# Second copy buffer in the gradient stage, four kernel-gradient rows, other places of loads, stores and jobs in a fused H3 and SiLU training step

## The chip, the cores and the metric

The kernel runs on one core of a Trainium2 chip. A core has a matrix engine (TensorE, in the profile PE, its weight loads PEld), a vector engine (VectorE, DVE), a scalar engine (ScalarE, ACT), GpSimd (POOL) and SyncE (SP), which here only issues DMAs. Each engine works through its own instructions in order; semaphores tie the engines together. DMAs are issued from the queues of SP, ACT and POOL and share 16 DMA engines. The metric is the device time of one execution in microseconds; lower is better.

## The reference

It is a forward pass of two layers and its vector-Jacobian product, with S = 2048 rows, D = 448 channels and F = 1792 hidden channels, in bfloat16:

```python
def _A_ref(q, k, v, shift_k, ssm_k, ssm_D):        # sequence mixing
    k_shift = sum(k_pad[:, t:t+S] * shift_k[:, ks-1-t] for t in range(4))
    kv = k_shift * v
    y = irfft(rfft(pad(kv)) * rfft(pad(ssm_k)))[:S] + kv * ssm_D
    return q * y
def _B_ref(x, w1, w2):                             # dense layer
    return silu(x @ w1) @ w2
x = A_q
for layer in range(2):
    x = x + _A_ref(_layernorm(x), A_k, A_v, A_shift_k, A_ssm_k, A_ssm_D)
    x = x + _B_ref(_layernorm(x), B_w1, B_w2)
```

This is shortened; the layer norm has no weights. The outputs are `x` and the gradients, for a given `grad_out`, of `q`, `k`, `v`, `shift_k`, `ssm_k`, `ssm_D`, `w1` and `w2`. The convolution's result `y` is the same in both layers, since `k`, `v` and the kernels are.

## The kernel before, in words

The work has three parts.

The prefix, `_ssm_prefix` (about the first 100 us), computes `y`: a Fourier transform of length 4096 as two stages of matmuls with constant matrices (`M1s`, `Gsb`, `Minvs`). It leaves the spectra in HBM (`spec_K`, `spec_KV`) and `y` in SBUF. `Gsb` is loaded once, into a pool that lives as long as the kernel.

The middle, `Main.run`, works in chunks `c` of 512 rows, four in each layer. Forward layer 0 comes first, then a loop over layer 1's chunks that does the second half of `h` (the product with `w1`, L518 through `contract`), `out` (the product with `w2`, L600), and then already the backward part of the same chunk. Then comes a loop over layer 0's chunks with the backward part only. The backward part of a chunk has two functions:

- `ga` (L618) makes the gradient that goes through `w2`. In seven pairs of F tiles `fp`, TensorE runs 8 matmuls of 512 columns into the tile `ps_g`, ACT copies it to SBUF as `ghp` (L626), and DVE multiplies `ghp` by the slope of SiLU, `dT`, into `ghT` (L634). `ps_g` has two buffers, `ghp` one. `mid` and `slope` put further ACT or DVE work between the pairs.
- `gn` (L662) runs 56 matmuls `ps_n` with `w1T` (L672), which ACT moves out as `lb_u` (L674), and then the backward pass of two layer norms (`ln_bwd`, lines 640 to 660), almost all of it on DVE (`lb_junk`, `lb_cc`, `lb_u`, `G`, `gy`), with `lb_v` on ACT (L652).

At the head of a chunk stands `g_pre`. It loads the output gradient `gb` (in layer 1, from SP's queue) and transposes it on TensorE into `gT`. In `contract` the argument `at` decides whether the half-height blocks of a product stand first or last: it is compared with 0 only.

The suffix, `_ssm_suffix`, does two things at once. It runs the sequence mixing backwards: stage 1 of the transform (`_fft_stage1`, 16 columns `n2`, moved out as `A1g`, the first twelve on ACT), transposes, spectra (`spectrum`, `inverse`), the gradient of `ssm_k` (L969 to L993: four rows `gK` of 112 channels, each made by two groups of 16 matmuls, copied by ACT or DVE, then stored), that of `k` and `v` (L998 on), and the sums for `gk` on DVE. Between these, it weaves the *jobs*, the weight gradients: 56 jobs of 16 matmuls `ps_d` (L808), each of which loads a tile `dstat` of 512 KB on SP's queue. `weave(n)` puts `n` job matmuls between two steps of the transform, and `_in_turn` keeps TensorE's order as written. A pair of jobs makes one tile of 128 rows: `_gw2` for `w2` (moved out as `dout`, stored from POOL's queue, L823), `_gw1` for `w1` (also transposed, `do`, L835 to L838). Where the weaving is over, the rest of the jobs follow one another to the end.

The order inside each engine's queue is decided by a scheduler when the program is built: it may draw an instruction ahead of others when its data and buffers allow, unless the code pins it (`issue_after`, `_in_turn`, `high_priority`). A pool's tile with a `tag` and `bufs=n` takes turns among `n` places; a new tile waits until the last reader of the old one in its place is done. `k.bal` keeps a running estimate of the loads of ACT and DVE and gives a copy to the one with less.

Of the kernel before, what the change touches and what calls it, by code (L numbers as in the profile page):

```python
# [10 lines left out]
FP32 = mybir.dt.float32  # L11
# [108 lines left out]
@with_exitstack  # L120
def kernel(
    ctx: ExitStack,
    tc: tile.TileContext,
    A_q: bass.AP,
    A_k: bass.AP,
    A_v: bass.AP,
    A_shift_k: bass.AP,
    A_ssm_k: bass.AP,
    A_ssm_D: bass.AP,
    B_x: bass.AP,  # L130
    B_w1: bass.AP,
    B_w2: bass.AP,
    grad_out: bass.AP,
    out_0: bass.AP,
    out_1: bass.AP,
    out_2: bass.AP,
    out_3: bass.AP,
    out_4: bass.AP,
    out_5: bass.AP,
    out_6: bass.AP,  # L140
    out_7: bass.AP,
    out_8: bass.AP,
):
    nc = tc.nc
    k = K()
    k.tc, k.nc = tc, nc
    k.bal = _Bal(nc)
    for nm, v in (("A_q", A_q), ("A_k", A_k), ("A_v", A_v), ("A_shift_k", A_shift_k), ("A_ssm_k", A_ssm_k),
                  ("A_ssm_D", A_ssm_D), ("B_w1", B_w1), ("B_w2", B_w2), ("grad_out", grad_out)):
        setattr(k, nm, v)  # L150
    k.outs = [out_0, out_1, out_2, out_3, out_4, out_5, out_6, out_7, out_8]
    C = make_fft_consts()

    dram = ctx.enter_context(tc.tile_pool(name="dram", bufs=1, space=DRAM))
    k.KS_d = dram.tile([S, D], BF16, name="KS_d")
    k.SPEC_d = {nm: dram.tile([128, SPEC], BF16, name=f"spec_{nm}") for nm in ("K", "KV")}
    k.N_d = [dram.tile([S, D], BF16, name=f"N_d{i}") for i in range(4)]
    k.DT_d = dram.tile([4, 2, P, NF // 2, 512], BF16, name="DT_d")
    k.A_d = [dram.tile([P, NF, NT, P], BF16, name=f"A_d{i}") for i in range(2)]
    k.AP_d = dram.tile([4, P, S], BF16, name="AP_d")  # L160
    k.GH_d = [dram.tile([P, NF, NT, P], BF16, name=f"GH_d{i}") for i in range(2)]

    bf = mybir.dt.np(BF16)
    m1b = np.ascontiguousarray(C["M1"], dtype=np.float32).astype(bf)
    minv = (np.transpose(m1b.astype(np.float32), (3, 1, 2, 0)) * np.float32(C["inv_scale"])).astype(bf)
    k.m1_h = nc.inline_tensor(np.ascontiguousarray(m1b.reshape(P, -1)), name="c_m1")
    gs_h = nc.inline_tensor(np.ascontiguousarray(C["Gs"].reshape(P, -1)).astype(np.float32).astype(bf), name="c_gs")
    k.minv_h = nc.inline_tensor(np.ascontiguousarray(minv.reshape(P, -1)), name="c_minv")

    keep = ctx.enter_context(tc.tile_pool(name="keep", bufs=1))  # L170
    k.ident = keep.tile([P, P], BF16, name="ident")
    make_identity(nc, k.ident[:])
    k.Gsb = keep.tile([P, 5, P], BF16, name="Gsb")
    nc.gpsimd.dma_start(out=k.Gsb[:].rearrange("p a k -> p (a k)"), in_=gs_h.ap())
    k.rstd = [keep.tile([P, J], FP32, name=f"rstd{i}") for i in range(4)]
    k.warm = keep.tile([P, 4], FP32, name="warm")
    k.mhalf = keep.tile([P, 4], FP32, name="mhalf")
    nc.gpsimd.memset(k.mhalf[:], -0.5)
    nc.scalar.activation(k.warm[:], k.mhalf[:], ACT.Silu)
    k.wk = ctx.enter_context(tc.tile_pool(name="wk", bufs=1))  # L180
    k.dp = ctx.enter_context(tc.tile_pool(name="dp", bufs=1))
    k.yk = ctx.enter_context(tc.tile_pool(name="yk", bufs=1, side="right", reuse_waits="tile"))
    k.Ysb = k.yk.tile([P, J, D], BF16, name="Ysb", tag="Y")
    _ssm_prefix(k)
    k.w1sb = k.wk.tile([P, ND, F], BF16, name="w1sb", tag="WA")
    nc.sync.dma_start(out=k.w1sb[:, 0:3, :], in_=k.B_w1[0:384].rearrange("(c p) f -> p c f", p=P))
    nc.sync.dma_start(out=k.w1sb[:, 3, :], in_=k.B_w1[320:448])
    k.w2sb = k.wk.tile([P, NF, D], BF16, name="w2sb", tag="WB")
    nc.sync.dma_start(out=k.w2sb[:], in_=k.B_w2.rearrange("(c p) d -> p c d", p=P))
    k.psum = ctx.enter_context(tc.tile_pool(name="psum", bufs=1, space=PSUM, reuse_waits="tile"))  # L190
    k.xg = ctx.enter_context(tc.tile_pool(name="xg", bufs=1, side="right", reuse_waits="tile"))
    k.X = k.xg.tile([P, NT, D], BF16, name="X", tag="X")
    k.gYb = k.xg.tile([P, NT, D], BF16, name="gYb", tag="GY")
    k.bal.reset()
    with ExitStack() as es:
        m = Main(k, es)
        m.run()
    _ssm_suffix(k)


# [80 lines left out]
def _ssm_prefix(k):  # L281
# [4 lines left out]
    with ExitStack() as es:  # L286
# [22 lines left out]
        skc = spec.tile([DC, ND, 4], FP32, name="skc")  # L309
        skb = spec.tile([DC, ND, 4], BF16, name="skb")  # L310
        Drow = spec.tile([1, D], BF16, name="Drow")

        nc.gpsimd.dma_start(out=Drow[:], in_=k.A_ssm_D.rearrange("(o d) -> o d", o=1))
        nc.scalar.dma_start(out=skb[:], in_=k.A_shift_k.rearrange("(c p) j -> p c j", p=DC))
# [149 lines left out]
class Main:  # L464
# [98 lines left out]
    def h(self, c, L, nT, half, hold, pre=None):  # L563
# [2 lines left out]
        dT = self.td.tile([P, NF // 2, 512], BF16, name="dT", tag="D", bufs=3)  # L566
        hold.append((aT, dT))
        d0 = pre() if pre else None
        for ft0, n, at in ((0, 2, 1), (2, 2, 0), (4, 2, None), (6, 1, None)) if half == 0 else ((7, 1, None), (8, 2, 1), (10, 2, 0), (12, 2, None)):
            ps = k.psum.tile([P, 2, 512], FP32, name="ps_h", tag="mm", bufs=2)  # L570
            self.contract(ps, self.w1sb, nT, ft0, n, at)
            o = ft0 - 7 * half
# [30 lines left out]
        if last:  # L603
            nc.gpsimd.dma_start(out=_pm(k.outs[0][0])[:, 4 * c:4 * c + 4, :], in_=X[:, 4 * c:4 * c + 4, :])

    def g_pre(self, c, L):
        nc, k = self.nc, self.k
        sl = slice(4 * c, 4 * c + 4)
        if L == 1:
            gb = self.ch.tile([P, 4, D], BF16, name="gb", tag="gb", bufs=2)  # L610
            nc.sync.dma_start(out=gb[:], in_=_pm(k.grad_out[0])[:, sl, :])
        else:
            gb = k.X[:, sl, :]
        gT = self.ch.tile([P, ND, 512], BF16, name="gT", tag="nT", bufs=2)
        self.transp(gb, gT)
        return gb, gT

    def ga(self, c, L, gT, dT, mid=None, loads=(None, None)):  # L618
# [3 lines left out]
        for fp in range(NF // 2):  # L622
            ps = k.psum.tile([P, 2, 512], FP32, name="ps_g", tag="mm", bufs=2)
            self.contract(ps, self.w2T, gT, 2 * fp, 2, None if fp == 6 else (fp + 1) % 2)
            gh = self.ch.tile([P, 2, 512], BF16, name="ghp", tag="ghp", bufs=1)
            k.last_gh = nc.scalar.copy(gh[:], ps[:])  # L626
            k.bal.add("act", 0.95)
            k.bal.add("dve", -0.5)
# [84 lines left out]
    def run(self):  # L713
# [19 lines left out]
            self.out(c, cur, False)  # L733
            cur = fol
        for c in range(4):
            gb, gT = self.g_pre(c, 1)
            d0 = self.h(c, 1, nT, 1, cur, (lambda: self.load_d(0, 0)) if c == 3 else None)
            if c < 3:
                na1 = self.a_fwd(c + 1, 2, None)
# [1 line left out]
            if c < 2:  # L741
                self.turn_plain(2 * c)
                self.turn_plain(2 * c + 1)
            if c == 3:
                self.slope(d0)
            box = []
# [79 lines left out]
def _gw1(k, pool, slots):  # L826
# [5 lines left out]
    def turn(ft, o):  # L832
        pt = psum.tile([DC, ND, P], BF16, name="ps_dt", tag="po", bufs=2)
        for dc in range(ND):
            nc.tensor.transpose(pt[:, dc, :], o[:, dc * DC:(dc + 1) * DC], k.ident[:])  # L835
        o7 = pool.tile([DC, ND, P], BF16, name="do7", tag="do7", bufs=2)
        nc.scalar.copy(o7[:], pt[:])
        nc.gpsimd.dma_start(out=out7v[:, :, ft * P:(ft + 1) * P], in_=o7[:])  # L838

    hold = None  # L840
    for ft in range(NF):
# [15 lines left out]
def _ssm_suffix(k):  # L857
# [6 lines left out]
    k.pt = dict(s1=mm, s2=mm, v=mm)  # L864
    with ExitStack() as es:
        pool = lambda name: es.enter_context(tc.tile_pool(name=name, bufs=1, reuse_waits="tile"))
        sp = pool("sspec")
        k.Minvsb = sp.tile([P, 16, 2, P], BF16, name="Minvs")
        dp2 = pool("dp2")
        k.tail = None  # L870
        both = [(k.dp, "dstat", 3), (k.dp, "dstat", 3), (dp2, "dstat", 2), (k.dp, "dstat", 3), (dp2, "dstat", 2)]
        for _ in _gw2(k, k.dp, range(1), [(k.dp, "dstat", 3)], first=k.go_jobs.ins):
            pass

        def jobs():
            yield from _gw2(k, k.dp, range(1, 4), [(k.dp, "dstat", 3)])
            yield from _gw2(k, k.dp, range(4, NF), both)
            yield from _gw1(k, dp2, both)

        jobs = jobs()  # L880
# [1 line left out]
        def weave(n):  # L882
            with _in_turn(k):
                for _ in zip(range(n), jobs):
                    pass
        A1 = sp.tile([P, NDH, 2, 16, 4], BF16, name="A1g")
        Z = sp.tile([P, NDH, P], BF16, name="Zg")
        ksf = k.yk.tile([P, J, D], BF16, name="ksf", tag="Y")
        B1k = A1[:].rearrange("p a c n s -> p (a c n s)").rearrange("p (q d) -> p q d", d=D)
        for n2 in range(16):  # L890
            with _in_turn(k):
                _fft_stage1(k, n2, k.gYb[:, n2, :], A1, psum, nc.scalar if n2 < 12 else None)
            weave(4 if n2 < 8 else 8 if n2 < 11 else 10)
        with tc.tile_pool(name="sspec2", bufs=1, reuse_waits="tile") as p1:
            Zf = Z[:].rearrange("p a b -> p (a b)")
            A1f = A1[:].rearrange("p a c n s -> p a (c n s)")
# [64 lines left out]
        for lo, hi in ((1, 113), (113, 128)):  # L961
            nc.scalar.dma_start(out=kx[lo:hi, 0:3, :], in_=k_pm[lo - 1:hi - 1, 13:16, :])
        nc.gpsimd.memset(gkh[:], 0.0)
        sk_all = p2.tile([P, D * 4], BF16, name="sk_all2", tag="gK", bufs=2)
        nc.sync.dma_start(out=sk_all[:], in_=k.A_shift_k.rearrange("d j -> (d j)").partition_broadcast(P))
        skb = p2.tile([P, 4, D], BF16, name="skb2")
        nc.vector.tensor_copy(skb[:], sk_all[:].rearrange("p (d j) -> p j d", j=4))
# [2 lines left out]
        pr = psum.tile([1, ND, DC], FP32, name="ps_r", tag="po", bufs=2)  # L970
        gKs = []
        for dc in range(ND):
            gK = p2.tile([DC, S], BF16, name="gK", tag="gK", bufs=2)
            gKv = gK[:].rearrange("p (n1 n2) -> p n1 n2", n2=16)
            for g in range(2):
                py = psum.tile([P, 8, P], FP32, name="ps_gK", **mm)
# [69 lines left out]
            nc.gpsimd.dma_start(out=o4[1536:1792].rearrange("(b n) -> b n", b=2), in_=gsk[0:2, 3, :])  # L1046
        weave(2 * NF * 2 * NT)
        for g in range(8):
            acc = p2.tile([P, 2, D], FP32, name="gk_acc", tag="gK", bufs=2)
            gk = p2.tile([P, 2, D], BF16, name="gk", tag="gk", bufs=2)  # L1050
            last = None
            for j in range(4):
# [41 lines left out]
```

## Time and profile before

| | us |
|---|---|
| median of 8 runs (lowest to highest) | 770.17 (769.1 to 773.7) |
| the profiled execution | 773.7 |
| its span, first to last instruction | 771.9 |
| TensorE busy | 715.3 (93%) |
| VectorE busy | 509.7 (66%) |
| ScalarE busy | 457.0 (59%) |
| GpSimd busy | 102.5 (13%) |
| chain that ended last | TensorE 36%, VectorE 27%, issue 15%, ScalarE 11%, DMA 6% |
| output gradient `gb`, issue to landing | 4.7 (4 loads of 448 KB, SP) |
| store of a `gK` row, issue to landing | 6.1 (4 stores, POOL) |

In a row of a timeline the first number is the start in the span, the second the duration of the group of instructions, then come the engine, the line, the operation, the result and the operands with their shapes, and the count. In brackets stands how long the engine had been idle just before and what ended that. In a row of the waits stand the engine, tile and line that waited, the one it waited for, the sum in us, how many times, and the longest. TensorE's matmuls are pipelined, so the duration of a group is a little longer than its distance from the next.

### The profile page before, as it was taken

How to read it: one execution, taken by the hardware profiler on the slowest of the kernel's cores; microseconds unless marked ns; L12 is line 12 of the kernel's file. 1: busy time of each engine (PE TensorE's matmuls, PEld its weight loads, DVE VectorE, ACT ScalarE, POOL GpSimd, SP SyncE). 2: the span in 40 equal slices, each digit the busy share in tenths (PEclk: the TensorE clock that was granted, in tenths of full speed). 3: DMA queues.
4: the chain of work that ended last, by engine and by line, in shares of the span. 5: the costliest groups of instructions: out<-in, count | busy, mean ns of one | idle time of the engine just before them, and what ended most of it. 6: DMA issues, size and time to landing. Idle time of an engine off the chain costs nothing.

```text
span 771.9 us, 12680 instructions
## 1 busy us (share of the span) xinstructions
PE 715.3 (93%) x4981; PEld 382.1 (50%) x5025; DVE 509.7 (66%) x1061; ACT 457.0 (59%) x574; POOL 102.5 (13%) x169
## 2 busy tenths in 40 slices
PE   5998779999999999999999999999999989799995
PEld 4876534444444443434444344344666765455553
DVE  3789758788733796966949778886487715169600
ACT  3878867666557587578857678647467645011111
POOL 1134312222100001000000000002011123021111
PEclk9999979999999999999999999999999999899998
DMA  9449989999979998859889999998669786487760
GB/s 291 162 142 275 362 247 307 263 295 266 214 164 236 216 234 206 178 146 250 193 177 274 285 233 274 283 240 296 246 222 354 259 285 205 125 275 230 220 180 18
DMA packets 187623, 180.01 MB, mean 233 GB/s; under 512 B 135242, under 2 KB 163790, under 8 KB 186412
## 3 DMA queue, kind: packets, MB, share of 16 engines
q1 hardware_dynamic: 173808, 121.98, 61.1%
q0 software_dynamic: 12832, 54.70, 20.6%
q10 hardware_dynamic: 924, 2.52, 1.0%
q8 instruction: 39, 0.64, 0.3%
q14 instruction: 20, 0.16, 0.1%
HBM read 76.50 MB, written 65.87 MB: 184 GB/s over the span
## 4 chain that ended last, share of the span: by engine, by line
PE 36%; DVE 27%; issue 15%; ACT 11%; DMA 6%; POOL 3%; SPq 0%; ACTq 0%; POOLq 0%; DVEq 0%
PE ps_d L808 9%; PE ps_o L600 7%; PE ps_h L518 6%; DVE lb_junk L647 4%; DVE dT L113 3%; DVE ghT L634 3%; DVE lb_u L658 3%; ACT ghp L626 3%; PE ps_v L233 2%; DVE lb_u L687 2%; PE ps_n L672 2%; PE ps_v L232 2%; ACT na L274 2%; DVE ln_st L260 2%; DMA KB<-Z 1%
## 5 line engine op out<-in xcount | busy, mean ns | idle before, releaser
L808 PEld LDWEIGHTS <-dstat 128*128 128x128 bf16 x896 | 85.6, 98 | 74.0 <-issue 3.1
L518 PE MATMUL ps_h<-nT,w1sb 128*128 128x512 bf16 (+1 forms) x434 | 102.9, 386 | 5.9 <-DVE dT L113 3.1
L518 PE MATMUL ps_g<-gT,w2T 128*128 128x512 bf16 (+1 forms) x431 | 97.4, 380 | 9.1 <-ACT ghp L626 7.1
L672 PE MATMUL ps_n<-w1T,ghT 128*128 128x448 bf16 x448 | 92.6, 353 | 1.0 <-DVE ghT L634 0.4
L600 PE MATMUL ps_o<-w2sb,aT 128*128 128x448 bf16 x448 | 90.8, 353 | 0.2 <-ACT aT L575 0.2
L808 PE MATMUL ps_d<-mov,dstat 128*128 128x448 bf16 x448 | 87.4, 353 | 0.2 <-DMA mov<-N_d 0.2
L575 ACT ACTIVATE aT<-ps_h 128x1024 bf16<-128x1024 f32 (+1 forms) x64 | 58.2, 917 | 41.3 <-PE ps_h L518 32.6
L626 ACT CAST ghp<-ps_g 128x1024 bf16<-128x1024 f32 x56 | 56.5, 1008 | 37.0 <-DVE ghT L634 22.9
L113 DVE CAST dT<-ps_h 128x1024 bf16<-128x1024 f32 (+1 forms) x56 | 59.2, 1064 | 26.5 <-ACT aT L575 26.5
L518 PEld LDWEIGHTS <-w2T 128*128 128x128 bf16 (+1 forms) x448 | 36.4, 96 | 68.1 <-issue 37.5
L518 PEld LDWEIGHTS <-w1sb 128*128 128x128 bf16 (+1 forms) x448 | 36.5, 97 | 67.8 <-issue 40.0
L672 PEld LDWEIGHTS <-ghT 128*128 128x128 bf16 x448 | 41.5, 98 | 45.4 <-DVE ghT L634 5.7
L600 PEld LDWEIGHTS <-aT 128*128 128x128 bf16 x448 | 42.1, 98 | 42.6 <-issue 4.5
L808 PE MATMUL ps_d<-X,dstat 128*128 128x448 bf16 x224 | 53.5, 364 | 0.1
L808 PE MATMUL ps_d<-GO,dstat 128*128 128x448 bf16 x224 | 51.2, 352 | 0.2
L232 PE MATMUL ps_v<-Gsb,pa 128*128 128x128 bf16 x336 | 43.8, 221 | 5.4 <-DVE pa L442 4.7
L233 PE MATMUL ps_v<-Gsb,pb 128*128 128x128 bf16 x336 | 42.9, 222 | 2.3 <-DVE pb L942 1.1
L852 ACT CAST dout<-ps_d 128x448 bf16<-128x448 f32 x14 | 7.4, 532 | 58.7 <-PE ps_d L808 58.7
L232 PEld LDWEIGHTS <-pa 128*128 128x128 bf16 x336 | 33.2, 99 | 10.5 <-DVE pa L442 6.8
L674 ACT ACTIVATE lb_u<-ps_n,rstd 128x448 f32<-128x448 f32 x32 | 20.3, 634 | 29.6 <-DVE X L659 13.5
L233 PEld LDWEIGHTS <-pb 128*128 128x128 bf16 x336 | 32.9, 99 | 9.3 <-DVE pb L443 4.6
L634 DVE TENSOR_TENSOR ghT<-dT,ghp 128x1024 bf16<-128x1024 bf16 (+1 forms) x32 | 19.5, 620 | 26.9 <-ACT ghp L626 26.9
(189 smaller groups left out, 1172.6 us busy)
## 6 DMA issues: line engine op xcount, KB each, us to landing
GH_d<-turned SPq DMA_DIRECT2D x16, 896.0 KB, 5.4
dstat<-A_d SPq DMA_DIRECT2D x28, 512.0 KB, 5.2
dstat<-GH_d SPq DMA_DIRECT2D x28, 512.0 KB, 3.8
A_d<-turned SPq DMA_DIRECT2D x12, 896.0 KB, 4.6
DT_d<-dT POOLq DMA_DIRECT2D x8, 896.0 KB, 6.0
dTl<-DT_d SPq DMA_DIRECT2D x8, 896.0 KB, 6.3
spec_K<-Z POOLq DMA_DIRECT2D x7, 512.0 KB, 7.6
KB<-Z POOLq DMA_DIRECT2D x14, 256.0 KB, 12.2
```

The source lines that it names most:

```text
L113: eng.tensor_copy(out, in_)
L232: nc.tensor.matmul(pv[:, i, :], lhsT=pa[:, i * P:(i + 1) * P], rhs=k.Gsb[:, ga, :], start=True, stop=False)
L233: nc.tensor.matmul(pv[:, i, :], lhsT=pb[:, i * P:(i + 1) * P], rhs=k.Gsb[:, gb, :], start=False, stop=True)
L518: self.nc.tensor.matmul(ps[:, u, :], lhsT=w[lo:hi, b, f:f + P], rhs=x[lo:hi, b, :], start=(seen[u] == 1), stop=(seen[u] == ND))
L575: last = nc.scalar.activation(a, ps[:, 0:n, :], ACT.Silu)
L600: nc.tensor.matmul(po[:, :D], lhsT=aT[ft // 7][0][:, ft % 7, tl * P:(tl + 1) * P], rhs=self.w2sb[:, ft, :], start=(ft == 0), stop=(ft == N ...
L626: k.last_gh = nc.scalar.copy(gh[:], ps[:])
L634: nc.vector.tensor_tensor(out=ghT[hh][:, o:o + len(u), :], in0=dT[hh][1][:, o:o + len(u), :], in1=gh[:, u[0]:u[0] + len(u), :], op=ALU.mult)
L647: nc.vector.scalar_tensor_tensor(out=junk[:], in0=u0, scalar=1.0, in1=n_t, op0=ALU.mult, op1=ALU.mult, accum_out=cp[:, 1:2])
L658: nc.vector.scalar_tensor_tensor(out=u0, in0=n_t, scalar=cc[:, 1:2], in1=u0, op0=ALU.mult, op1=ALU.add)
L672: nc.tensor.matmul(pn[:, :D], lhsT=ghT[ft // 7][:, ft % 7, tl * P:(tl + 1) * P], rhs=self.w1T[:, ft, :], start=(ft == 0), stop=(ft == NF - 1))
L808: i = k.nc.tensor.matmul(ps[:, :D], lhsT=st[:, t, :], rhs=mov[:, t, :], start=start and t == 0, stop=stop and t == NT - 1)
```

## The change

1. `Gsb` no longer lives as long as the kernel: the prefix loads it into its own pool, and the suffix loads it again (`Gs`), in both cases from POOL's queue.
2. `h` passes `at` as 1 where it passed None.
3. The load of the output gradient becomes a function, `g_load`; layer 1's loop calls it for the next chunk ahead of `ga`, and for the first ahead of the loop's work.
4. `ghp` has two buffers.
5. The last two stores of `w1`'s gradient are issued on SP's queue.
6. In the suffix the pool `dp2` is laid out first, `Minvs` and `Gs` after `A1g`; the jobs rotate over five `dstat` tiles (three in `k.dp`, two in `dp2`) from the second pair on, where that began with the fifth pair.
7. Stage 1 weaves 2 job matmuls after each of columns 0 to 7, 8 after 8 to 11, and 12 after 12 to 15, in all 96, where it had 4, 8 (up to column 10) and 10, in all 106.
8. The tag `gK` (the rows `gK`, before them `sk_all`, after them `gk_acc`) has four places.

```diff
-    k.Gsb = keep.tile([P, 5, P], BF16, name="Gsb")
-    nc.gpsimd.dma_start(out=k.Gsb[:].rearrange("p a k -> p (a k)"), in_=gs_h.ap())
+    k.gs_h = gs_h
...
+        k.Gsb = spec.tile([P, 5, P], BF16, name="Gsb")
+        nc.gpsimd.dma_start(out=k.Gsb[:].rearrange("p a k -> p (a k)"), in_=k.gs_h.ap())
...
-        for ft0, n, at in ((0, 2, 1), (2, 2, 0), (4, 2, None), (6, 1, None)) if half == 0 else ((7, 1, None), (8, 2, 1), (10, 2, 0), (12, 2, None)):
+        for ft0, n, at in ((0, 2, 1), (2, 2, 0), (4, 2, 1), (6, 1, 1)) if half == 0 else ((7, 1, 1), (8, 2, 1), (10, 2, 0), (12, 2, 1)):
...
-    def g_pre(self, c, L):
+    def g_load(self, c):
+        gb = self.ch.tile([P, 4, D], BF16, name="gb", tag="gb", bufs=2)
+        self.nc.sync.dma_start(out=gb[:], in_=_pm(self.k.grad_out[0])[:, 4 * c:4 * c + 4, :])
+        return gb
+
+    def g_pre(self, c, L, gb=None):
         nc, k = self.nc, self.k
-        sl = slice(4 * c, 4 * c + 4)
-        if L == 1:
-            gb = self.ch.tile([P, 4, D], BF16, name="gb", tag="gb", bufs=2)
-            nc.sync.dma_start(out=gb[:], in_=_pm(k.grad_out[0])[:, sl, :])
-        else:
-            gb = k.X[:, sl, :]
+        if L == 0:
+            gb = k.X[:, 4 * c:4 * c + 4, :]
...
-            gh = self.ch.tile([P, 2, 512], BF16, name="ghp", tag="ghp", bufs=1)
+            gh = self.ch.tile([P, 2, 512], BF16, name="ghp", tag="ghp", bufs=2)
...
-            gb, gT = self.g_pre(c, 1)
+            gb, gT = self.g_pre(c, 1, gb_next if c else self.g_load(0))
...
+            if c < 3:
+                gb_next = self.g_load(c + 1)
             if c == 3:
                 self.slope(d0)
...
-        nc.gpsimd.dma_start(out=out7v[:, :, ft * P:(ft + 1) * P], in_=o7[:])
+        (nc.gpsimd if ft < NF - 2 else nc.sync).dma_start(out=out7v[:, :, ft * P:(ft + 1) * P], in_=o7[:])
...
+        dp2 = pool("dp2")
         sp = pool("sspec")
-        k.Minvsb = sp.tile([P, 16, 2, P], BF16, name="Minvs")
-        dp2 = pool("dp2")
...
-            yield from _gw2(k, k.dp, range(1, 4), [(k.dp, "dstat", 3)])
-            yield from _gw2(k, k.dp, range(4, NF), both)
+            yield from _gw2(k, k.dp, range(1, NF), both)
...
         A1 = sp.tile([P, NDH, 2, 16, 4], BF16, name="A1g")
+        k.Minvsb = sp.tile([P, 16, 2, P], BF16, name="Minvs")
+        k.Gsb = sp.tile([P, 5, P], BF16, name="Gs")
+        nc.gpsimd.dma_start(out=k.Gsb[:].rearrange("p a k -> p (a k)"), in_=k.gs_h.ap())
...
-            weave(4 if n2 < 8 else 8 if n2 < 11 else 10)
+            weave(2 if n2 < 8 else 8 if n2 < 12 else 12)
...
-        sk_all = p2.tile([P, D * 4], BF16, name="sk_all2", tag="gK", bufs=2)
+        sk_all = p2.tile([P, D * 4], BF16, name="sk_all2", tag="gK", bufs=4)
...
-            gK = p2.tile([DC, S], BF16, name="gK", tag="gK", bufs=2)
+            gK = p2.tile([DC, S], BF16, name="gK", tag="gK", bufs=4)
...
-            acc = p2.tile([P, 2, D], FP32, name="gk_acc", tag="gK", bufs=2)
+            acc = p2.tile([P, 2, D], FP32, name="gk_acc", tag="gK", bufs=4)
```

## The prediction

> **What bounds the kernel now.** I read the engine shares first, then the waits, then the stages in which TensorE waits.
>
> ```profile
> PE 715.3 (93%) x4981; PEld 382.1 (50%) x5025; DVE 509.7 (66%) x1061; ACT 457.0 (59%) x574; POOL 102.5 (13%) x169
> ```
>
> TensorE is busy for 715.3 of 771.9 us, so without less work for it at most 56.6 us can be recovered, and some 20 of these lie in the first 110 us, which the change leaves alone. The waits:
>
> ```profile
> DVE ghT L634 <- ACT ghp L626: 36.6, 29, 3.0
> ACT ghp L626 <- DVE ghT L634: 22.9, 26, 2.5
> PE ps_g L518 <- ACT ghp L626: 7.1, 18, 1.4
> ```
>
> (us in total, times, longest.) With one `ghp` buffer, copy and multiply take turns: copy 1.01, multiply 0.69, a period of about 1.8. In layer 1's last chunk TensorE runs 54 of these matmuls in 12.05 us, hence 1.72 per pair of tiles, without a wait: there the alternation costs nothing. It costs where ACT and DVE also hold `gn`'s work, in the layer-0 loop:
>
> ```profile
> 452.93 0.69 DVE L634 TENSOR_TENSOR ghT<-dTl,ghp 128x1024 bf16<-128x1024 bf16 x1 [0.50 <-ACT ghp L626]
> 454.75 0.69 DVE L634 TENSOR_TENSOR ghT<-dTl,ghp 128x1024 bf16<-128x1024 bf16 x1 [1.13 <-ACT ghp L626]
> 456.72 0.69 DVE L634 TENSOR_TENSOR ghT<-dTl,ghp 128x1024 bf16<-128x1024 bf16 x1 [1.28 <-ACT ghp L626]
> 458.87 0.62 DVE L647 SCALAR_TENSOR_TENSOR lb_junk<-lb_u,nb_l 128x448 bf16<-128x448 f32 x1 [1.46 <-ACT lb_u L674]
> ```
>
> The last row opens a chunk's `gn` on DVE. From 450.6 to there DVE does some 2.5 us of work in 8.2. The same row comes at 402.10, 430.50, 458.87, 486.91 and 513.35, so a chunk takes 28.4, 28.4, 28.0 and 26.4 us. By the windows between them DVE is busy for 24.2, 22.9, 22.9 and 22.8, TensorE for 26.2, 25.9, 26.6 and 25.3 (of it 3.7 and 3.15 are 17 and 14 weight-gradient matmuls of the last two): neither fills the period; the turn-taking does.
>
> The second place is the kernel-gradient stage. TensorE:
>
> ```profile
> 632.43 1.06 PE L981 MATMUL ps_gK<-Minvs,A1g 128*112 128x128 bf16 x16
> 636.62 1.73 PE L981 MATMUL ps_gK<-Minvs,A1g 128*112 128x128 bf16 x16 [2.57 <-ACT gK L111]
> 638.14 1.32 PE L808 MATMUL ps_d<-X,dstat 128*128 128x448 bf16 x3
> 639.26 1.51 PE L981 MATMUL ps_gK<-Minvs,A1g 128*112 128x128 bf16 x16
> ```
>
> and ACT, whose copy holds it up:
>
> ```profile
> 635.55 1.01 ACT L111 CAST gK<-ps_gK 112x1024 bf16<-112x1024 f32 x1 [5.71 <-DMA out_dram<-gK]
> ```
>
> The row to be copied must wait until an earlier row has left its buffer; the chain of what ended last has that store as one piece of 8.69 us.
>
> **The change, part by part.**
>
> *Kernel gradient, tag gK from two to four.* The 2.57 us of idle go. The matmuls behind also run slow: 16 take 1.73 and 1.51 instead of 1.06, and three jobs 1.32 instead of 0.73. That is 0.67 + 0.59 + 0.45 = 1.7; the granted clock of 635–638 and 638–641 is 0.80 and 0.63. The Trainium skill ("TensorE: Matmul & The Clock Gate", section "Why this matters for your kernels") says that one idle window of about 3 us brings half clock, so by it a gap of 2.57 costs only itself: a gain of 2.6. The trace shows the clock lower after 2.57, so I take the rows: −4.2. The fourth row reuses the place of `sk_all`, free once `skb` is copied; that copy began at 626.75, after its DMA, and lasted 1.10, ahead of the fourth row's at about 632.
>
> *Two copy buffers.* Fixed is the multiplies' order; a copy can now run during the multiply before it. In the tail above the first two copies would be done early (waits of 0.50 and 1.13 gone). The last two follow on ACT at 1.0 each behind `lb_v` (0.76) and the `gT` copy (1.01), and the last multiply still has 8 matmuls and an `lb_u` (0.63) behind it. I make 8.2 into about 6.1: 2.1 per chunk. The first loop transition comes from layer 1's last chunk, where only part applies: 3.5 × 2.1 = −7.4. Bounds: 0, if the copies come no earlier because ACT itself is late; and −14.9, if layer 0's chunks fall to their work: matmul counts by their steady times (0.215, 0.188, transposes 0.066) give 25.7 and 25.0 for the first two, DVE's 22.9 and 22.8 bind the others, 96.4 against 111.25. In layer 1, TensorE's waits for `ghp` are about 2 of the 7.1; I take −1.5 (bounds 0, −2). The other 5 lie in the tails already counted.
>
> *The first job moves.* The built order puts its 32 matmuls in one block behind the last `ps_n`, where before 31 lay inside layer 0's last two chunks. Steady they cost 32 × 0.189 = +6.05 in a stage that TensorE bounds. They did not lengthen the chunks that held them (28.0 with 17, 28.4 without), so nothing is returned twice.
>
> *Stage 1 with two jobs per column instead of four.* Before:
>
> ```profile
> 524.82 0.54 PE L212 MATMUL ps_s<-gYb,M1s 128*128 128x448 bf16 x2
> 525.20 0.92 PE L808 MATMUL ps_d<-GO,dstat 128*128 128x448 bf16 x4
> 529.18 0.54 PE L212 MATMUL ps_s<-gYb,M1s 128*128 128x448 bf16 x2 [0.79 <-ACT A1g L111]
> ```
>
> and ACT:
>
> ```profile
> 525.71 0.91 ACT L111 CAST A1g<-ps_s 128x896 bf16<-128x896 f32 x1
> ```
>
> One column took TensorE 1.14 (0.38 and 0.76), so the copy of 0.91 kept up. With two jobs it takes 0.76 and ACT sets the pace: 8 × 0.15 = 1.2, and ACT also has `lb_u` (0.85) and `lb_v` (0.76) among the copies where only 0.6 of slack is left. I estimate 3.3 of idle against 0.9: +2.4 (bounds 0, if the block of 32 lets ACT finish first, and 4). The matmuls taken from here run later; their number is the same.
>
> *The tail.* The last two stores go from POOL's queue to SP's. The last on POOL:
>
> ```profile
> 765.52 0.71 POOL L838 DMA_DIRECT2D out_dram<-do  x1 [4.94 <-ACT do L837]
> ```
>
> SP's plain issues take 0.32 to 0.9, and its queue is empty by then; the landing (2.5 to 5.2, median 3.4) stays. The Trainium skill ("DMA: Bandwidth & Descriptors", section "Specifications") gives first-byte latencies of about 1 us from GpSimd's path and 0.6 from SP's: an estimate of −0.4, of which no row here shows anything. By the issue rows alone the move makes −0.4 to +0.2, with the estimate −0.8 to −0.2; I take −0.5 and keep +0.2 and −0.8 as bounds.
>
> *ACT's table loads.* The order has two more (1.28 each) around layer 1's slopes. ACT is 59% busy, so they are mostly covered; without cover 2.6. I take +0.5.
>
> *Costed at nothing.* `h`'s `at` of 1 for None: `contract` asks only whether it is 0, so the same matmuls come in the same order. The `gb` loads: in the built order the four stand where they stood in SP's queue, since the scheduler had already hoisted them (issue 0.92, landing 4.7); were one late, `gT`'s transposes and all of `ga` behind it on TensorE would be, by at most 5.6. `Gsb` is loaded twice: one more POOL issue of 0.54 ahead of the first `dout` store and of the `kk_c` loads; POOL had idled 5.91 and 12.89 before such stores, and the tile is needed some 40 us later. If that cover were gone, `kk_c` would be 0.54 late and the spectrum with it. Five tiles from the beginning put SP's loads slightly ahead; TensorE waited just 0.2 for a job's data in all, so more has nothing to give.
>
> **The sum**: −4.2 − 7.4 − 1.5 + 6.05 + 2.4 − 0.5 + 0.5 = −4.65. The profiled span of 771.9 would be 767.2 and its run, 773.7, 769.0. That run was the highest of the eight shown (769.1 to 773.7), 3.5 above their median; from the median 770.17 the forecast is 765.5. With the loop's return between 6 and 9.5 in all and the small terms at their ends, its own range is 762 to 768.5.
>
> **The rivals.**
>
> *Slower: layer 0 gives nothing back.* If ACT is late for reasons of its own (at 449 to 451 it was copying `gT` for 1.94 while `ghp` waited), the second buffer stands empty and only the suffix's bill is left: 6.05 + 2.4 + 0.5 − 4.2 − 0.5 = +4.25, so 774.4; at 0.4 per chunk, 772.8, which I take. It decides when the loops together return under 4.25, some 1.1 a chunk. For it: DVE works without a break for about 20 us of each chunk. Against: the 36.6 us in which DVE waited for just this copy.
>
> *A transfer takes the place of the gK wait.* DMA is full there (share 0.99, 0.96, 1.03 from 626 to 635). Should `sk_all`, the fourth row's place, or the jobs' data come some 4 us late, that gain is spent: 765.5 + 4.2 = 769.7. For it: `skb` had waited 7.50 for `sk_all`'s DMA. Against: its copy ended 4 us before it would be needed.
>
> *More than forecast.* Without turn-taking layer 0 falls to near its engines' work, with 1.2 of stalls left per chunk: −10 for −7.4, and the block of 32 gives ACT the time to clear, so stage 1 costs nothing: 765.5 − 2.6 − 2.4 = 760.5.
>
> *It doesn't do what it says*: true of the loads and of `at`, and in the sum.
>
> **How the numbers follow.** The forecast 0.46, more 0.15, transfer 0.16, slower 0.23. What a measurement of this kernel can tell from no change is about 0.2%, 1.5 us: 768.7 to 771.7. Faster: 0.46 + 0.15 + 0.02 of the transfer case = 0.63. Same: 0.14 of the transfer and 0.03 of the slower = 0.17. Slower 0.20. The range goes from 759, below the case of more, to 773.5, past the slower case's 772.8; what is left out is about 0.18.
>
> **What would show it.** Right: DVE's waits for `ghp` at 10 to 20 in place of 36.6; chunks of 26 to 26.5; no wait of `gK` for its store and a clock of 1.00 there; 32 jobs without a gap before stage 1, then waits of TensorE for `A1g`. Wrong: chunks still at 28, or a new wait of TensorE for `dstat` or `Minvs` behind the gK stage.

## The result

The changed kernel took 765.27 us, the median of 11 runs, against 770.45 for the kernel before in 32. One of the 11 was a slow execution (783.0), and the ratio, taken from the means of the fast ones, is 0.9917 (95% interval 0.9896 to 0.9937), 6.4 us faster, where the medians differ by 5.2. The forecast was 765.5 with a range of 759 to 773.5, so total and sign held. The sum behind them held only in part: two of its terms are about right (layer 0, the block of 32 matmuls), two are right in size but mean something else (the kernel gradient, stage 1), and two are off by 3 to 5 us in opposite directions (the tail, layer 1). The experiments are mostly about that.

The waits of the changed kernel's trace (who waited for whom; us in total, times, longest):

```profile
DVE ghT L636 <- ACT ghp L628: 22.3, 19, 3.1
...
PE ps_t L530 <- ACT gT L111: 4.8, 2, 4.6
...
PE ps_g L519 <- ACT ghp L628: 3.3, 4, 1.1
...
PE ps_s L211 <- ACT A1g L111: 2.0, 3, 1.1
...
PE ps_d L812 <- DMA dstat<-A_d: 1.2, 1, 1.2
```

DVE's wait for `ghp` fell from 36.6 to 22.3 and TensorE's from 7.1 to 3.3. The 22.3 is still above the 10 to 20 that I had named as a sign of being right. The second line is new: 4.8, where it was at most 0.7 with one buffer. The rows of VectorE that open the chunks of layer 0 (and the last of layer 1):

```profile
402.00 0.62 DVE L649 SCALAR_TENSOR_TENSOR lb_junk<-lb_u,nb 128x448 bf16<-128x448 f32 x1 [2.66 <-ACT lb_u L676]
...
428.29 0.63 DVE L649 SCALAR_TENSOR_TENSOR lb_junk<-lb_u,nb_l 128x448 bf16<-128x448 f32 x1 [1.94 <-ACT lb_u L676]
...
454.51 0.62 DVE L649 SCALAR_TENSOR_TENSOR lb_junk<-lb_u,nb_l 128x448 bf16<-128x448 f32 x1 [1.40 <-ACT lb_u L676]
...
479.98 0.62 DVE L649 SCALAR_TENSOR_TENSOR lb_junk<-lb_u,nb_l 128x448 bf16<-128x448 f32 x1 [1.44 <-ACT lb_u L676]
...
503.89 0.63 DVE L649 SCALAR_TENSOR_TENSOR lb_junk<-lb_u,nb_l 128x448 bf16<-128x448 f32 x1 [0.22 <-ACT lb_u L676]
```

The chunks take 26.3, 26.2, 25.5 and 23.9 us instead of 28.4, 28.4, 28.0 and 26.4. TensorE in the kernel-gradient stage, where a wait of 2.57 stood and groups of 16 took 1.73 and 1.51:

```profile
631.71 1.06 PE L986 MATMUL ps_gK<-Minvs,A1g 128*112 128x128 bf16 x16
...
633.17 1.06 PE L986 MATMUL ps_gK<-Minvs,A1g 128*112 128x128 bf16 x16
```

No wait, 1.06 each, and a granted clock of 1.00 from 630 to 636. TensorE in stage 1, behind the block of 32 matmuls that ends at 515.7:

```profile
519.71 0.54 PE L211 MATMUL ps_s<-gYb,M1s 128*128 128x448 bf16 x2 [1.06 <-ACT A1g L111]
...
524.45 0.54 PE L211 MATMUL ps_s<-gYb,M1s 128*128 128x448 bf16 x2 [0.59 <-ACT A1g L111]
526.23 1.69 PE L812 MATMUL ps_d<-GO,dstat 128*128 128x448 bf16 x8 [1.24 <-DMA dstat<-A_d]
```

Three waits for `A1g` (with one of 0.32) and one for the data of a job.

The two first profiles are a poor pair, one some 3 us above its median, the other some 5 below. So the table sets a second profile of each side by side, `again` (before, a run of 766.7) and `same` (changed, 760.4), both close to their medians. Each row is a stretch between the same two instructions in both.

| stretch, from the start of one to the start of the next | before | changed | difference |
|---|---|---|---|
| start to first `ps_n` | 247.9 | 248.1 | +0.2 |
| to the last of layer 1's chunks (its `lb_junk`) | 150.4 | 154.0 | +3.6 |
| to the last chunk of layer 0 | 111.3 | 101.9 | −9.4 |
| to the first `ps_tr` of the suffix (the block, stage 1) | 32.8 | 40.1 | +7.2 |
| to the kernel gradient | 76.7 | 76.7 | 0 |
| to `ps_gkv` | 20.2 | 16.1 | −4.1 |
| to `ps_sk` | 15.2 | 15.2 | 0 |
| to the last `ps_dt` | 102.8 | 102.4 | −0.4 |
| to the end of the span | 7.6 | 3.8 | −3.8 |

The sum is −6.7, the spans are 764.9 and 758.3. The rows differ in work, too: in the one up to the first `ps_tr` of the suffix the changed kernel runs 128 matmuls of jobs, before 108, since 30 of the first job came here from layer 0 and 10 of stage 1 left; these 10 (1.9 us) run in the stretch to the last `ps_dt`, with 488 for 478.

### The profile page after: what moved, and what is told of

It reads as the page before. It is cut to its first block, busy times and chain, and to the rows that moved or that the text cites. A ratio compares the mean times of both kernels' runs of the same rounds, so it can differ in the third digit from the quotient of the medians.

```text
span 758.4 us, 12686 instructions
## 1 busy us (share of the span) xinstructions
PE 704.8 (93%) x4980; PEld 378.5 (50%) x5025; DVE 509.8 (67%) x1061; ACT 459.4 (61%) x576; POOL 101.1 (13%) x168
## 4 chain that ended last, share of the span: by engine, by line
PE 53%; DVE 23%; ACT 11%; DMA 5%; issue 5%; POOL 1%; SPq 0%; ACTq 0%; DVEq 0%; POOLq 0%
PE ps_d L812 20%; PE ps_o L601 7%; PE ps_h L519 7%; DVE lb_junk L649 3%; PE ps_n L674 3%; DVE dT L113 2%; DVE lb_u L660 2%; PE ps_g L519 2%; DVE ghT L636 2%; PE ps_v L232 2%; PE ps_v L231 2%; ACT na L273 2%; DVE ln_st L259 2%; DVE lb_u L689 2%; DMA KB<-Z 1%
## 5 line engine op out<-in xcount | busy, mean ns | idle before, releaser
L519 PE MATMUL ps_g<-gT,w2T 128*128 128x512 bf16 (+1 forms) x432 | 92.4, 380 | 4.9 <-ACT ghp L628 3.3
L674 PE MATMUL ps_n<-w1T,ghT 128*128 128x448 bf16 x448 | 89.5, 353 | 3.9 <-DVE ghT L636 3.7
L812 PE MATMUL ps_d<-X,dstat 128*128 128x448 bf16 x224 | 50.9, 352 | 0.1
L561 ACT ACTIVATE dTl<-dTl 128x1024 bf16<-128x1024 bf16 (+1 forms) x32 | 28.6, 940 | 6.7 <-DMA dTl<-DT_d 6.7
L602 DVE TENSOR_TENSOR X<-X,ps_o 128x448 bf16<-128x448 bf16 x32 | 19.6, 614 | 16.4 <-PE ps_o L601 16.4
```

What stands on the lines that cost most here:

```text
L519: self.nc.tensor.matmul(ps[:, u, :], lhsT=w[lo:hi, b, f:f + P], rhs=x[lo:hi, b, :], start=(seen[u] == 1), stop=(seen[u] == ND))
L561: self.nc.scalar.activation(d[:, o:o + n, :], d[:, o:o + n, :], ACT.Derivative_silu)
L674: nc.tensor.matmul(pn[:, :D], lhsT=ghT[ft // 7][:, ft % 7, tl * P:(tl + 1) * P], rhs=self.w1T[:, ft, :], start=(ft == 0), stop=(ft == NF - 1))
L812: i = k.nc.tensor.matmul(ps[:, :D], lhsT=st[:, t, :], rhs=mov[:, t, :], start=start and t == 0, stop=stop and t == NT - 1)
```

## The experiments

All ratios are to the kernel before on the same chip; 0.001 is 0.77 us. The differences to the changed kernel are differences of these ratios, mostly to the 0.9921 of its second set of runs (`same`, below); with intervals of about ±0.002 each, such a difference is known to about 2 us. The runs stand in the order of what they answer.

**Does the profile of before repeat?** The kernel unchanged.

> The kernel before, unchanged, profiled once more. It tells what of its first profile repeats. My theory: the layer-0 chunks of 28.4, 28.4, 28.0 and 26.4 us, the wait of 2.57 us in the kernel-gradient stage and the slower clock behind it come again, since they follow from buffers. Rival: the gap of 4.04 us among the ps_sk matmuls (661.4 to 665.5) and the 6.7 us from the last copy to the end of the span were that one execution's own and do not repeat, and with them goes most of its 3.5 us above the median. Time 770.2 +-1 by both.

0.9989 (0.9975 to 1.0003). The chunks, the waits for `ghp` (36.6 again) and the wait for `gK` (2.36, clock 0.58 around it) repeat. The gap among the `ps_sk` matmuls repeats smaller, 2.4 for 4.0, and the long end of the span repeats exactly, against the rival.

**The second buffer, undone.**

```diff
-            gh = self.ch.tile([P, 2, 512], BF16, name="ghp", tag="ghp", bufs=2)
+            gh = self.ch.tile([P, 2, 512], BF16, name="ghp", tag="ghp", bufs=1)
```

> The changed kernel with one ghp buffer again; all other parts as changed. By the built order, the first job's 32 matmuls go back between layer 0's chunks. My theory (the loop returned 8.9 us by the second buffer, at 6.05 of moved matmuls): 765.3 + 8.9 - 6.05 = 768.1, chunks of about 28 again and DVE's waits for ghp near 36. Rival (the shorter chunks are only the matmuls that left them): 765.3 within 1.0. Second rival (the buffer alone carries all of the gain, and the moved matmuls cost nothing in the suffix): 772 or more.

0.9896 (0.9875 to 0.9918): no theory had it; by the ratios it is some 2 us *faster* than the changed kernel, with intervals that overlap. So the second buffer, with all that it brings along, gained nothing that these runs show. The first job's 32 matmuls went back between layer 0's chunks, which took 28.4, 28.4, 28.1 and 26.5.

**The moved matmuls alone.** One buffer, and the first job held where the changed kernel has it:

```diff
+                k.last_n = nc.tensor.matmul(pn[:, :D], ...).ins
...
+            if k.block:
+                es.enter_context(k.tc.issue_after(k.last_n))
             i = k.nc.tensor.matmul(ps[:, :D], lhsT=st[:, t, :], rhs=mov[:, t, :], ...)
```

(`k.block` is set for the first pair of jobs only.)

> The changed kernel with one ghp buffer, but with the first job's 32 matmuls held behind the last ps_n, as they stand in the changed kernel. Against the run ghp1 it gives the price of the moved matmuls, against the changed kernel that of the buffer. My theory: the moved matmuls cost their 6.05 in full, so 768.1 + 6.05 = 774.2. Rival (layer 0's last two chunks shorten as much as the suffix grows, because TensorE's work was in their way): the same as ghp1 within 1, near 768, with the third and fourth chunk some 3 us shorter than in ghp1.

0.9969 (0.9955 to 0.9983). Against ghp1 that is 5.3 us by the medians on the same chip, close to 32 × 0.189 = 6.05; layer 0's chunks did not shorten (28.4, 28.4, 28.8, 26.4), so the rival falls. Against the changed kernel (0.9917, and 0.9921 below) the second buffer, at the same place of these matmuls, is worth about 4 us. Layer 0's four chunks alone differ by 112.0 − 101.9 = 10.1. Some 6 us of what it gains there is lost elsewhere. By the stretches of the table, 3.6 of it are lost in layer 1 (154.0, in block 150.4) and 2.8 between the last chunk and the first `ps_tr` (40.1, in block 37.2), where the changed kernel waits 2.0 for `A1g` and 1.2 for `dstat`; block's trace has one wait there:

```profile
PE ps_s L211 <- ACT A1g L111: 1.1, 1, 1.1
```

**Where the buffer's gain goes.** TensorE in layer 1's last chunk, the changed kernel:

```profile
369.30 1.01 PE L530 MATMUL ps_t<-ident,gb 128*128 128x128 bf16 x8 [4.63 <-ACT gT L111]
```

ScalarE, which should have copied `gT`:

```profile
357.77 1.28 ACT L561 ACT_TABLE_LOAD   x1
365.74 1.06 ACT L561 ACTIVATE dTl<-dTl 128x1024 bf16<-128x1024 bf16 x1 [6.68 <-DMA dTl<-DT_d]
...
368.25 1.00 ACT L111 COPY gT<-ps_t 128x1024 bf16<-128x1024 bf16 x1
```

and SyncE's queue:

```profile
355.33 0.36 SPq L487 DMA_DIRECT2D GH_d<-turned  x1
355.79 4.68 SPq L485 DMA_TRANSPOSE turned<-aT  x1
360.53 0.57 SPq L698 DMA_DIRECT2D dTl<-DT_d  x1
```

The same queue in ghp1, and ScalarE's first slope there:

```profile
354.36 0.85 SPq L698 DMA_DIRECT2D dTl<-DT_d  x1
356.63 0.36 SPq L487 DMA_DIRECT2D GH_d<-turned  x1
357.09 7.06 SPq L485 DMA_TRANSPOSE turned<-aT  x2
```

```profile
359.74 1.06 ACT L561 ACTIVATE dTl<-dTl 128x1024 bf16<-128x1024 bf16 x1 [0.94 <-DMA dTl<-DT_d]
```

With two buffers the scheduler puts the load of `dTl` behind the store of `GH_d` and a DMA transpose of `aT`, where it stood ahead of these. It is issued some 6 us later in the chunk; the slope of `dTl` waits 6.68 for it at the head of ScalarE's queue, where it waited 0.94, and `lb_u` and `gT` stand behind. To test it, the slope was held behind the chunk's last SiLU (`k.last_h`), so that `lb_u` and `gT` no longer stand behind it:

```diff
             if c == 3:
-                self.slope(d0)
+                with self.tc.issue_after(k.last_h):
+                    self.slope(d0)
```

> The changed kernel itself, so that the runs beside it have it on the same chip, and its trace once more. By all theories 0.992 of the kernel before; the new wait of TensorE for gT in layer 1's last chunk (4.63 us in its first trace) comes again if it follows from the order on SP's queue, and not if it was that execution's own.

0.9921 (0.99 to 0.9942); TensorE's wait is there again, 5.4 us.

> The changed kernel, with layer 1's last slope (of the first tile dTl for layer 0) held on ScalarE behind the chunk's last SiLU. In the changed kernel this slope stands ahead of lb_u and gT on ScalarE and waits 6.7 us for its load, which has slipped behind a DMA transpose on SP. Theory after the first runs (the second buffer took back 4 to 5 us through that wait): 4 us faster than the changed kernel, 0.987 of the kernel before, and the wait of TensorE for gT gone. Rival (the time lost there is caught up before layer 0, where VectorE sets the pace): as the changed kernel, 0.992.

0.9843 (0.9824 to 0.9861), 6.0 us faster than the changed kernel on the same chip: the load still stands behind the transpose, and nobody waits for it. TensorE's line, the same in the run after this one:

```profile
PE ps_t L530 <- ACT gT L111: 0.2, 1, 0.2
```

The 6.0 is more than the 4 expected. Four of the table loads that ScalarE makes between SiLUs and slopes (1.28 each; 11 become 7) go as well, and how the 6.0 divide between the two was not tried.

**The first job back in layer 0's loop**, with slope's edit:

```diff
+            if L == 0 and fp == 5 and c:
+                for _ in zip(range(5), k.job0):
+                    pass
             ps = k.psum.tile([P, 2, 512], FP32, name="ps_g", tag="mm", bufs=2)
...
+            if c:
+                for _ in zip(range(6), k.job0):
+                    pass
             self.gn(c, 0, ghT, nb, ...)
```

(`k.job0` yields the first job's matmuls one by one; what is left of them runs where the whole job stood.)

> As the run slope, and the first job's 32 matmuls are written into layer 0's chunks 1 to 3 at the places where TensorE waited for ghp or ghT (5 before the sixth product of ga, 6 before gn). In the changed kernel TensorE has 1.8 to 2.2 us idle in each of these chunks, room for some 10 matmuls of 0.189. Theory (they cost nothing there, 5.3 in the suffix by the runs block and ghp1): 5 us faster than slope, 0.980. Rival (they lengthen the chunks, because the waits stand at other places by then): 0.987, as slope.

0.9799 (0.978 to 0.9817), 750.73 us: the fastest of the kernels here up to this run, 3.3 us better than slope. The other 2 us of the price are still paid: its chunks take 26.3, 25.9, 26.9 and 25.2, together 104.2 against 101.9, so the matmuls fit only in part. Layer 1 takes 146.9 in this trace, from the first `ps_n` to its last chunk's `lb_junk`: 7.1 less than in `same` and 3.5 less than before.

**The kernel gradient, undone** (three `bufs=4` of the tag `gK` back to 2; the order of every engine is unchanged).

> The changed kernel with two places for the tag gK again; the built order of every engine is that of the changed kernel. My theory: the wait of TensorE for the copy of gK comes back with the slower clock behind it, 765.3 + 4.2 = 769.5. By the clock gate's rule alone (a gap of 2.6 costs only itself): 767.9. Rival (the stall is taken up behind it, by a wait that stands there anyway): 765.3 within 1.

0.9943 (0.9921 to 0.9965), by the ratios some 2 us slower than the changed kernel, with intervals that overlap; the trace is the better witness. TensorE:

```profile
634.09 1.05 PE L986 MATMUL ps_gK<-Minvs,A1g 128*112 128x128 bf16 x16 [1.85 <-ACT gK L111]
```

and 3 us of each with all engines (after the stretch and its length: TensorE's, weight loads', VectorE's, ScalarE's and GpSimd's busy times, then TensorE's clock), gk2 first:

```profile
632.00:635.00 3.00, 1.15 (x19) 0.93 (x18) 0.00 (x0) 1.93 (x2) 0.00 (x0) 1.00 0.71 288
```

```profile
632.00:635.00 3.00, 2.37 (x18) 1.95 (x18) 0.00 (x0) 2.35 (x4) 1.12 (x2) 0.58 0.33 126
```

The wait comes back, but as 1.85, and the clock stays at 1.00; in again it is 2.36 with a clock of 0.58 in this stretch. The stage is 18.1 us in gk2, 16.1 in the changed kernel, 20.2 before. So the 4.2 is what stood there before; what the two places more are worth inside the changed kernel is 2. The gap there costs itself and nothing more; in the kernel before, the slow matmuls behind it added 1.7.

**The tail.** The last two stores back on POOL's queue (the expression for the engine becomes `nc.gpsimd`), and the same edit alone in the kernel before.

> The changed kernel, with the last two stores on POOL's queue again; nothing else moves in the built order. The prediction put the move at 0.5 us, so 0.9924 of the kernel before. Rival, from the traces (from the last copy's end to the end of the span 6.7 us before, 3.0 after): 3.8 us slower than the changed kernel, 0.9966.

0.9986 (0.9966 to 1.0006), 5.0 us slower than the changed kernel.

> The kernel before, with the last two stores of w1's gradient on SP's queue and nothing else; the other engines' order is unchanged. The prediction's step: -0.5 us, 0.9994. Theory after the run tailpool (the last bytes from POOL's queue are followed by some 3 us of nothing that the trace shows, those from SP's by 1): -3.8 us, 0.995.

0.9937 (0.9912 to 0.9962), 4.8 us faster than the kernel before. So this edit alone, of two stores' queue, is worth some 5 us (2.9 to 6.8 by sptail's interval). The last issue in again (before) and in same (changed), each with the window of 2 us in which its bytes end (last columns: DMA share, GB/s):

```profile
758.52 0.71 POOL L838 DMA_DIRECT2D out_dram<-do  x1 [4.94 <-ACT do L837]
```

```profile
760.00:762.00 2.00, 0.00 (x0) 0.00 (x0) 0.00 (x0) 0.00 (x0) 0.00 (x0) 0.50 0.12 29
762.00:764.00 2.00, 0.00 (x0) 0.00 (x0) 0.00 (x0) 0.00 (x0) 0.00 (x0) 0.50 0.00 0
```

```profile
755.39 0.32 SPq L842 DMA_DIRECT2D out_dram<-do  x1
```

```profile
756.00:758.00 2.00, 0.00 (x0) 0.00 (x0) 0.00 (x0) 0.00 (x0) 0.00 (x0) 0.50 0.29 57
```

In again the issue is at 758.5, the bytes end by 762, and the span ends at 764.9, 6.4 after the issue. In same these are 755.4, by 758, and 758.3: 2.9. Tailpool's trace has 6.4 again (754.07 to 760.5) and sptail's 2.9 (763.59 to 766.5). The 3.5 between are mostly time in which the trace of before shows nothing at all. That it belongs to POOL's queue is shown by the two runs; what happens in it is not.

**Stage 1's counts and the five tiles**, each undone.

```diff
-            weave(2 if n2 < 8 else 8 if n2 < 12 else 12)
+            weave(4 if n2 < 8 else 8 if n2 < 11 else 10)
```

> The changed kernel with the old counts of stage 1 (4, 8 from column 8, 10 from column 11). The prediction made ScalarE set stage 1's pace with two jobs per column, at +2.4 us: so this run would be 2.4 us faster than the changed kernel, 0.989. Rival (a job not woven here runs later at the same price and ScalarE's lateness comes from lb_v and lb_u, whatever the count): 0.992, no change. Second rival (with more jobs in stage 1 the loads of dstat come late, where the changed kernel already waits 1.24 us once): slower, 0.994.

0.9963 (0.9941 to 0.9985), 3.2 us slower than the changed kernel. TensorE:

```profile
520.81 0.54 PE L211 MATMUL ps_s<-gYb,M1s 128*128 128x448 bf16 x2 [0.42 <-ACT A1g L111]
...
527.31 1.67 PE L812 MATMUL ps_d<-GO,dstat 128*128 128x448 bf16 x4 [4.83 <-DMA dstat<-A_d]
```

The waits for `A1g` shrink from 2.0 to 0.4, as the prediction's mechanism has it, but the jobs arrive before their data: 4.83 for `dstat`, and slow matmuls behind (4 in 1.67, where 4 took 0.92).

```diff
-            yield from _gw2(k, k.dp, range(1, NF), both)
+            yield from _gw2(k, k.dp, range(1, 4), [(k.dp, "dstat", 3)])
+            yield from _gw2(k, k.dp, range(4, NF), both)
```

> The changed kernel with three places for dstat until the fourth pair of tiles, five from then on, as before. The prediction costed the five at nothing: 0.992, as the changed kernel. Rival (with the first job's matmuls out of layer 0's loop, stage 1 has too little time to load ahead, and the five are what keeps TensorE fed): slower by 2 us or more, 0.995, with waits of TensorE for dstat of some 3 us in stage 1.

0.9947 (0.993 to 0.9964), by the ratios 2.0 us slower, with intervals that just overlap. TensorE waits for `dstat` at two places, 2.9 in all instead of 1.2:

```profile
527.63 1.69 PE L812 MATMUL ps_d<-GO,dstat 128*128 128x448 bf16 x8 [1.11 <-DMA dstat<-A_d]
...
543.93 0.93 PE L812 MATMUL ps_d<-GO,dstat 128*128 128x448 bf16 x4 [1.75 <-DMA dstat<-A_d]
```

**Stage 1's old counts where the loads have a head start again**: the kernel `both`, with 4, 8 and 10.

> The kernel of the run both, with the old counts of stage 1 (4, 8, 10). There the first job's matmuls are back in layer 0's loop, so the loads of dstat have their old head start. The prediction's mechanism, alone: with four jobs per column TensorE takes 1.14 us to ScalarE's 0.91, the three waits for A1g of the run both (0.69, 0.51, 0.79) go, and the 10 matmuls more in this stage are 10 fewer at the end: 2 us faster than both, 0.977. Rival (dstat comes late here too, as in the run weave4): as both or slower, 0.980 to 0.984, with a wait of TensorE for dstat in stage 1.

0.9788 (0.9763 to 0.9813), 751.19 us: neither better nor worse than the kernel `both` by these intervals. The waits for `A1g` go from 2.0 to 0.5, and `dstat`, for which `both` did not wait, comes late once:

```profile
PE ps_d L821 <- DMA dstat<-A_d: 1.7, 1, 1.7
```

The one takes back the other.

## Why the prediction was right, and where it was not

**Kernel gradient, −4.2.** Right in its place: −4.1. The choice between the clock rule of the Trainium skill ("TensorE: Matmul & The Clock Gate", section "Why this matters for your kernels": half clock from gaps of about 3 us on) and the rows was right for the kernel before: the gap of 2.36 in its second profile has the slow clock behind it too, and one of 1.96 in sptail. As the price of the two places it was too high: undone inside the changed kernel it is 2, with full clock. What else in the change took the slow clock away there is open.

**Layer 0, −7.4.** The mechanism held and the size was low: −9.4 by the chunks, −10.1 against block, whose first job stands at the same place. I had counted three and a half transitions at 2.1; all four gained, 2.1 to 2.6 each. (VectorE's work in the 8.2 us that I looked at is 3.3 by the window, not 2.5; the estimate did not rest on it.)

**Layer 1, −1.5.** This step failed: +3.6. The waits that I had priced did go (TensorE's for `ghp` in layer 1, from 2.1 to 0.5), but I had not read where SP's loads stand in the new order. The two table loads, which I costed at +0.5 as covered, were the visible end of it: the order showed a slope between two SiLUs, and I did not ask what that slope itself waits for. The run slope shows what stood in the way, 6.0 us for the wait and four table loads together.

**The block, +6.05.** Right: 5.3.

**Stage 1, +2.4.** Right as a sum (3.2 of waits there against 0.8 to 0.9 before), and by luck: `A1g` gave 1.2 more, not 2.4, and the other 1.2 is a wait for `dstat` that I had not put there. As the price of the edit it was wrong: in the changed kernel the old counts cost 3.2 more (weave4), since the jobs' data is late, so there the edit to two jobs is a gain. "More has nothing to give", said of five tiles because TensorE had waited 0.2 for a job's data before, failed in the same way: inside the change they give about 2.0 (slots). The cover was time, and the change itself took it away. With the first job in its early place (ghp1) there is no wait for `dstat`, nor with the late place and the longer chunks (block); the waits come where the late place and the shorter chunks meet (0 to 1.2 in the traces with the changed kernel's order).

**The tail, −0.5.** Failed: −3.8 in the trace, 4.8 to 5.0 in the runs. I summed issue and landing, with 0.4 from the Trainium skill's first-byte latencies ("DMA: Bandwidth & Descriptors", section "Specifications"), and left out what lies between the landing and the end of the span. The page before showed it: the last POOL issue at 765.52 with 0.71, and the span's end at 771.9.

**The gap of `ps_sk`** (2.4 to 4.0 in the three profiles with the order of before, 1.5 to 2.6 in the others) was not in the sum. The `ps_sk` matmuls, gap included, took 7.1 us in again and 5.4 in same. No run tells which part did that, as the gap stays small when each part is undone alone; that is open.

**The parts costed at nothing** but for the tiles (`at`, the `gb` loads, the second load of `Gsb`) were not run alone; the trace after shows no wait of TensorE for `gb` or for `Gs`, and `ps_gK` no new one for `Minvs`.

The forecast's sum was −4.65, the table's is −6.7. With the ten matmuls counted where they left, the gains that I lacked are 2.0 in layer 0, 3.3 in the tail and 2.3 from `ps_sk` on; the loss that I did not see is 4.6 in layer 1, table loads included, and the rest is under 1. That most of it cancels is luck. Of the rivals, the slower one fell at its first step: the chunks did shorten. A transfer did take the place of a gain, but the load of `dTl` in layer 1, not one in the kernel-gradient stage.

## What to carry to other kernels

When a buffer is added, read the new order of the DMA queues and of ScalarE as closely as that of TensorE: a load that slips behind one DMA transpose can keep its reader waiting at the head of an engine's queue, which stops what stands behind and has nothing to do with it. A price of nothing holds only while its cover stays; ask of each cover whether another part of the same change removes it. And the end of the span is a stage of its own: compare the last issue with the end, not with the landing.

## What the hardware showed that I had not expected

- The span ended 6.4 us after the last issue of a store on POOL's queue, 2.9 after one on SP's, with the same 112 KB; moving the last two stores is worth 4.8 us (0.9937, in the kernel before alone).
- A load behind a store and a DMA transpose on SP's queue was issued some 6 us later than ahead of them; the transpose alone held the queue for 4.68 us.
- The clock after a gap in TensorE's work did not follow the gap's length alone. TensorE's kernel-gradient row in sptail (the kernel before, but for the tail), and the `ps_sk` rows behind their gap in again and both4:

```profile
635.26 1.81 PE L981 MATMUL ps_gK<-Minvs,A1g 128*112 128x128 bf16 x16 [1.96 <-ACT gK L111]
```

```profile
659.67 2.19 PE L1030 MATMUL ps_sk<-kx_s,gks 128*32 128x128 bf16 x47 [2.44 <-issue]
```

```profile
649.98 1.28 PE L1044 MATMUL ps_sk<-kx_s,gks 128*32 128x128 bf16 x47 [2.60 <-issue]
```

16 matmuls of the kernel gradient take 1.81 behind a gap of 1.96, where gk2 has 1.05 behind 1.85. 47 of `ps_sk` take 2.19 behind 2.44 (clock 0.50 from 660 to 662), but 1.28 behind 2.60 (clock 1.00 from 650 to 652). So a gap of about 2 us can already be dear and one of 2.6 free; what decides between them, these runs do not show. The stall of the kernel gradient cost 4.2 with the slow matmuls behind it in one kernel, and 1.9 without them in another.
